# Attention, dense layer and expert layer on one Trainium2 core: one copy of the rows, activations split from products, a fourth output tile, an earlier list stage, another start-up

## The chip, the cores and the metric

The kernel runs on one core of one Trainium2 (trn2) chip. The metric is the device time of one execution in microseconds (us); the median of the runs counts. Engines are named as in the profile: PE is TensorE (matmuls; PEld its weight loads), DVE is VectorE, ACT is ScalarE, POOL is GpSimd, SP is SyncE, which issues nearly all transfers.

## The reference

8 batches of 8 heads, 576 tokens, head size 64; then 4608 tokens of width 512.

```
k_p, v_p = k, v averaged over groups of 8 tokens            # 72 keys a head
attn = softmax(q @ k_p.T / 8) @ v_p                         # 4608 x 512 after joining heads
h = attn @ w_in;  g = where(h > 0, h, exp(min(h, 0)) - 1)   # 512 -> 2048
x = g @ w_out                                               # 2048 -> 512
e = argmax(x @ w_gate);  p = softmax(x @ w_gate)[e]         # 8 experts
out = p * (relu(x @ w1[e]) @ w2[e])                         # 512 -> 1024 -> 512, only expert e of each token
```

## The kernel before, in words

**Products in three terms.** Nearly every float32 factor is cut into a high part (a cast to fp32r) and a low part (the rest), and a product is three matmuls: high by high, low by high, high by low. The cuts are work for ACT (the cast) and DVE or POOL (the subtraction): `w_hi`, `w_lo` for the dense weights, `split` in `m_split` for the experts' weights, `hh`/`hl` for the experts' activations, `zh`/`zl` for gathered rows.

**Attention and dense layer** (about 0 to 1017 us). 12 blocks of 384 tokens go through 16 steps each; a step is 12 matmuls of 128x384 into `h` (`g1_mm`, line 442), the activation over ACT and DVE (`elu_a`, `elu_b`, `elu_c`; lines 452 to 467) and 9 matmuls of 128x512 into `y` (line 484). The attention of later tiles is placed between these by a table of slots: `at(n, slot, fn)` puts a call into step n at a named slot of `step`, and every engine follows the written order. At the start two blocks run interleaved while weights are loaded, decoded (`w_bits`, `w_lo`) and keys and values of the first batches are averaged (`prep_k`, `pool_sum`, `k_scale`; `prep_v2_pool` on POOL). When a block is done, its rows `yr` (512 values and a gate weight) are ready, its 24 gate products are spread over the following steps (`route_at`: a list of how many `r_logit` a step, with `r_gate_load` of the next row of the gate matrix on SP), then `r_top`, `r_weight` (softmax, and the rows are written to DRAM by SP), `r_place` (places in the experts' lists). For blocks 0 to 9 the rows are written twice, to `ybuf` and to `yfirst`; the first five expert units gather from `yfirst`, the later ones from `ybuf`.

**Expert stage** (about 1017 us to the end). The lists of tokens by expert are cut into units: D of 512 tokens (4 tiles of 128), S of 256, T of 128, U of 32. Main units are D0 to D7, T0, T1, S0, T2, four steps each (i = 0 to 3, a quarter of the hidden width); small U units go beside three of them. `mix(n)` writes one step. For a D unit: `m_g1`, 48 matmuls of 128x256 into two banks `mh` and, in the same function, the activations `hh` (ACT, line 1149) and `hl` (DVE, line 1150); `ahead(n)`, a planner that emits the loads (`m_load`: `w1st`, `w2st`, 512 KB each, on SP) and cuts (`m_split`: two ACT casts of 128x1024, two DVE subtractions) of the weights of coming steps as space comes free; `turn_rows`, transposes `zT` of the gathered rows of the next unit (line 1077) with `zh`/`zl`; `m_g2` of the step before (24 matmuls of 128x512 into four banks `my`, and after its last quarter the outputs `o`, scaled by the gate and scattered); `trans_late`, two more transposes; `ahead(n)` again; then the `chores` of the last block: `logits` (4 of its 24 products a step over six steps), `r_top`, `r_weight` (whose three `ybuf` writes SP issues), `r_count`, `r_put`, `lists_rest`, `lists_part`, and `index` (`m_index`: SP reads a value and issues small loads of row numbers). Output tiles `o` are a ring of 3 (line 1176 and after), and each is held until its scatter to `out` has landed.

Of the kernel before, what the change touches and what calls it, by code (L numbers as in the profile page):

```python
# [88 lines left out]
def fused_kernel(ctx: ExitStack, tc: tile.TileContext, q, k, v, w_in, w_out, w_gate, w1, w2, cst, out):  # L89
# [8 lines left out]
    yfirst = dpool.tile([NA, ROW], F32, name="yfirst")  # L98
# [136 lines left out]
    def w_lo(n, c):  # L235
        nc.vector.tensor_sub(w_half(n, c, 1), decs.pop((n, c)).bitcast(F32), w_half(n, c, 0))
        if f"dec{n}_{c}" in slot_w:
            w_free(f"dec{n}_{c}")
# [327 lines left out]
    def r_weight(blk):  # L566
        lg = lgs.pop(blk)
        mx, mb, eq = tops.pop(blk)
        yr = yrows[blk]
        pool = lpool["p"] if blk == NBLK - 1 else mrpool  # L570

        def small_tile(shape, tag, dtype=F32):
            return pool.tile(shape, dtype, tag=tag, name=f"{tag}{blk}")

        se = mrpool.tile([P, TB], F32, tag="rse", name=f"rse{blk}")
        nc.vector.tensor_reduce(se, lg, axis=AX.X, op=ALU.add)
        nc.vector.tensor_scalar_add(se, se, 1e-9)
# [12 lines left out]
        routed[blk] = oh, [small_tile([P, TB, NE], "rpe"), small_tile([P, TB], "rpf"), small_tile([P, TB], "rpi", I32)]  # L590
# [42 lines left out]

    def score_at(t, n, slot="pe_mid"):
# [7 lines left out]
        at(n, "end", s_norm, t)  # L642
# [23 lines left out]
    for b in range(2, B):  # L666
# [6 lines left out]
        for h in range(H):  # L673
            x = n0 - 5 + h if b > 2 else n0 - 4 + min(h, 6)
            at(x - 2, "end", v_load, b, h)
            at(x, "end", prep_v, b, h)

    for n, t in enumerate(range(TB, 2 * TB)):
# [7 lines left out]
        for hh in range(2):  # L686
            at(n + 1, "pe_mid", t_mm, t, hh)
            at(n + 1, "act_hi", t_copy, t, hh, (nc.scalar.copy, nc.vector.tensor_copy)[hh])
# [8 lines left out]
    for n in range(2):  # L697
        w = n + 1
        at(n, "dve_first", w_bits, w, 0)
        at(n, "act_hi", w_hi, w, 0)  # L700
        at(n, "bits", w_bits, w, 1)
        at(n, "bits", w_lo, w, 0)
        at(n, "act_end", w_hi, w, 1)
        at(n, "act_end", w_lo, w, 1)
# [25 lines left out]
    def route_at(blk, n0, per):  # L730
# [3 lines left out]
        for x in range(NE * TB):  # L734
            e, j = divmod(x, TB)
            at(n0 + n, ("dve_mid", "end", "end")[x - sum(per[:n])], r_logit, blk, e, j)
# [20 lines left out]
    def step(n):  # L757
# [6 lines left out]
        elu_a(blk, f)  # L764
        run(n, "act_hi")
# [22 lines left out]
    def first_block():  # L788
# [262 lines left out]
    def m_row(it, u):  # L1051
# [3 lines left out]
        else:  # L1055
# [4 lines left out]
            in_=(yfirst if early_rows(it) else ybuf)[:, :],  # L1060
# [3 lines left out]

    def zf_tag():
        k = turns["zf"] = 1 - turns.get("zf", 0)
        return ("yr", "wgb1")[k]

    def m_trans(it, u):
# [8 lines left out]
        if kind in "TU":  # L1078
            z = mrpool.tile([P, KC, P], F32, tag=zf_tag(), name=f"zf{kind}{s}")
# [50 lines left out]

    def m_g1(it, i):
# [21 lines left out]
    def m_g2(it, i):  # L1153
# [21 lines left out]
        w_free(*(x for x in w_done.pop((it, i)) if x in slot_w))  # L1175
        if i == 3:
            for u in range(nu):
                o = ring(pools[1], [P, DM], F32, "o", 3, f"o{kind}{s}_{u}")
# [36 lines left out]
    def u_trans(it):  # L1215
# [5 lines left out]
        hT = pools[1].tile([P, 2, P], F32, tag="uT", name=f"uTs{s}")  # L1221
# [3 lines left out]
    def u_g2(it):  # L1225
# [15 lines left out]
        o = pools[1].tile([P, P], F32, tag="uo", name=f"uo{s}")  # L1241
# [100 lines left out]
    def logits(n):  # L1342
        for x in range(4 * n, 4 * n + 4):
# [14 lines left out]
    def index(x):  # L1358
        for it in (main[x], side.get(x)):
            if it:  # L1360
                m_index(it)
                m_bound(it)

    def mix(n):
        k, i = seq[n]
        it = main[k]
        if n:
            m_g1(it, i)
            ahead(n)
        for it2, u in trans_at.get(n, ()):  # L1370
            turn_rows(it2, u)
        if n >= 1:
            k0, i0 = seq[n - 1]
            m_g2(main[k0], i0)
# [7 lines left out]
        if n == 14:  # L1382
            for x in range(KD, KD + 3):
                index(x)
            m_gather(side[KD])
        if k >= 4 and i == 1 and k + 4 < len(main):
            index(k + 4)

    ENGINES = {E.PE, E.Activation, E.DVE, E.Pool, E.SP}
    with tc.manual_schedule(engines=ENGINES):  # L1390
        m_g1(main[0], 0)
        for b2, f2 in pend:
            g2(b2, f2)
        y_evac(last)
# [3 lines left out]
    with tc.manual_schedule(engines=ENGINES):  # L1398
# [81 lines left out]
```

## Time and profile before

| | us |
|---|---|
| three runs | 1553.57, 1555.94, 1559.24 (median 1555.94) |
| the profiled execution | 1548.99, span 1547.1 |
| PE busy | 1431.8 (93%), x8834 |
| DVE busy | 969.3 (63%) |
| ACT busy | 739.2 (48%) |
| POOL busy | 127.3 (8%) |
| mean granted TensorE clock | 0.966 |

The span is the time from the first to the last instruction. PE works through its instructions in the written order, so that a wait of one matmul is a hole in the span; the waits of PE with what ended them, and the stretches with a lowered granted clock (1 is 2.4 GHz, 0.5 is 1.2 GHz), are what a change of the order of work can win or lose. A busy share of another engine says little by itself: DVE can be idle on average and late at one place.

### The profile page before, as it was taken

How to read it: one execution, taken by the hardware profiler on the slowest of the kernel's cores; microseconds unless marked ns; L12 is line 12 of the kernel's file. 1: busy time of each engine (PE TensorE's matmuls, PEld its weight loads, DVE VectorE, ACT ScalarE, POOL GpSimd, SP SyncE). 2: the span in 40 equal slices, each digit the busy share in tenths (PEclk: the TensorE clock that was granted, in tenths of full speed). 3: DMA queues.
4: the chain of work that ended last, by engine and by line, in shares of the span. 5: the costliest groups of instructions: out<-in, count | busy, mean ns of one | idle time of the engine just before them, and what ended most of it. 6: DMA issues, size and time to landing. Idle time of an engine off the chain costs nothing. (4 is left out here: it accounts for less than half of the span.)

```text
span 1547.1 us, 24285 instructions
## 1 busy us (share of the span) xinstructions
PE 1431.8 (93%) x8834; PEld 1254.1 (81%) x8834; DVE 969.3 (63%) x2235; ACT 739.2 (48%) x1778; POOL 127.3 (8%) x129
## 2 busy tenths in 40 slices
PE   7899889879999999999999999998888798898988
PEld 4698778768887888887888888897877697877877
DVE  7999777776675777685768576945444533324251
ACT  5677645345655555554656555622223223223241
POOL 1000000000000000000000000202012112112010
PEclk9899999999999999999999999999999899999999
DMA  9245225475545271736281625644464344747460
GB/s 291 73 156 191 87 72 81 95 99 65 77 85 69 81 90 55 79 85 71 72 94 54 75 42 62 179 87 132 128 174 105 101 167 158 247 153 263 158 204 26
DMA packets 108738, 177.27 MB, mean 115 GB/s; under 512 B 15101, under 2 KB 46335, under 8 KB 108608
## 3 DMA queue, kind: packets, MB, share of 16 engines
q1 hardware_dynamic: 101200, 155.65, 44.7%
q0 software_dynamic: 7408, 19.97, 3.9%
q8 instruction: 71, 1.16, 0.4%
q14 instruction: 59, 0.48, 0.2%
HBM read 146.28 MB, written 29.76 MB: 114 GB/s over the span
## 5 line engine op out<-in xcount | busy, mean ns | idle before, releaser
L484 PE MATMUL y<-woh,gh 128*128 128x512 f32 x576 | 235.4, 409 | 2.6 <-ACT yr L500 1.4
L484 PE MATMUL y<-wol,gh 128*128 128x512 f32 x576 | 228.6, 397 | 0.0
L484 PE MATMUL y<-woh,gl 128*128 128x512 f32 x576 | 228.2, 396 | 0.0
L442 PE MATMUL h<-xh,wih 128*128 128x384 f32 x768 | 174.3, 349 | 20.7 <-DVE g L460 19.1
L535 DVE SCALAR_TENSOR_TENSOR junk<-yr,wgb 128x512 bf16<-128x512 f32 x264 | 180.8, 685 | 18.1 <-DMA wgb<-in_moe_w_gate_dram 15.4
L459 DVE SCALAR_TENSOR_TENSOR g<-g,th 128x384 f32<-128x384 f32 x192 | 106.4, 554 | 112.8 <-ACT th L454 111.8
L466 ACT CAST gh<-g 128x384 fp32r<-128x384 f32 x192 | 98.8, 514 | 159.6 <-DVE g L460 141.0
L442 PEld LDWEIGHTS h<-xh,wih 128*128 128x128 f32 x768 | 138.9, 193 | 42.8 <-DVE g L460 21.2
L1149 ACT ACTIVATE hhD<-mhD 128x512 fp32r<-128x512 f32 x64 | 38.3, 598 | 277.9 <-PE myD L1168 269.8
L442 PE MATMUL h<-xl,wih 128*128 128x384 f32 x768 | 169.0, 343 | 0.0
L1150 DVE SCALAR_TENSOR_TENSOR hlD<-mhD,hhD 128x512 fp32r<-128x512 f32 x64 | 44.0, 690 | 198.4 <-ACT hhD L1149 190.9
L442 PE MATMUL h<-xh,wil 128*128 128x384 f32 x768 | 167.7, 341 | 0.0
L452 ACT ACTIVATE th<-h 128x384 f32<-128x384 f32 x192 | 94.3, 491 | 150.6 <-PE h L442 148.7
L442 PEld LDWEIGHTS h<-xl,wih 128*128 128x128 f32 x768 | 139.7, 193 | 0.2
L442 PEld LDWEIGHTS h<-xh,wil 128*128 128x128 f32 x768 | 139.6, 192 | 0.0
L467 DVE TENSOR_TENSOR gl<-g,gh 128x384 fp32r<-128x384 f32 x192 | 107.1, 558 | 42.8 <-ACT gh L466 38.1
L484 PEld LDWEIGHTS y<-woh,gl 128*128 128x128 f32 x576 | 108.8, 189 | 26.0
L484 PEld LDWEIGHTS y<-woh,gh 128*128 128x128 f32 x576 | 109.2, 190 | 24.5 <-DVE yr L502 2.0
L484 PEld LDWEIGHTS y<-wol,gh 128*128 128x128 f32 x576 | 109.1, 189 | 17.5
L611 POOL DMA_INDIRECT tab<-toki,rpi x36 | 37.4, 1039 | 932.8 <-DVE rpi L609 452.4
L1168 PE MATMUL myD<-m2hD,hhD 128*128 128x512 f32 x256 | 103.4, 404 | 7.9 <-DVE gateU L1074 2.9
L460 DVE TENSOR_TENSOR g<-g,h 128x384 f32<-128x384 f32 x192 | 106.3, 554 | 6.6
(272 smaller groups left out, 2483.2 us busy)
## 6 DMA issues: line engine op xcount, KB each, us to landing
wgb<-in_moe_w_gate_dram SPq DMA_DIRECT2D x96, 256.0 KB
w1stD<-in_moe_w_dram SPq DMA_DIRECT2D x32, 512.0 KB
w2stD<-in_moe_w_dram SPq DMA_DIRECT2D x32, 512.0 KB
kst<-in_k_dram SPq DMA_DIRECT2D x32, 288.0 KB
qT<-in_q_dram SPq DMA_DIRECT2D x36, 256.0 KB
ybuf<-yr SPq DMA_DIRECT2D x33, 256.5 KB
raw<-in_moe_w_in_dram SPq DMA_DIRECT2D x16, 512.0 KB
raw<-in_moe_w_out_dram SPq DMA_DIRECT2D x15, 512.0 KB
```

Of the source, the lines that this page charges most:

```text
L442: mark["g1"] = nc.tensor.matmul(ps, wi[i][a][:, c, o:o + P], bb[blk][:, c, :], start=n == 0, stop=n == 3 * KC - 1).ins
L452: nc.scalar.activation(th, hps[blk, f], AF.Relu, scale=-1.0)
L459: nc.vector.scalar_tensor_tensor(g, g, 1.0, th, op0=ALU.add, op1=ALU.mult)
L460: nc.vector.tensor_max(g, g, hps.pop((blk, f)))
L466: nc.scalar.copy(gh, g)
L467: nc.vector.tensor_sub(gl, g, gh)
L484: nc.tensor.matmul(ys[blk][j], a[:, js], wo[i][bb][:, o, :], start=n == 0 and f in FIRST[blk], stop=n == 2 and f in LAST[blk],)
L535: nc.vector.scalar_tensor_tensor(junk, yrows[blk][j][:, :DM], 1.0, pes[blk, e], op0=ALU.mult, op1=ALU.mult, accum_out=lgs[blk][:, j, e:e + 1])
L611: nc.gpsimd.indirect_dma_start(out=tab[:, :], out_offset=bass.IndirectOffsetOnAxis(ap=pi[:, j:j + 1], axis=0), in_=toki[:, TB * blk + j:TB ...
L1149: nc.scalar.activation(hh, ps, AF.Relu)
L1150: nc.vector.scalar_tensor_tensor(hl, ps, 0.0, hh, op0=ALU.max, op1=ALU.subtract)
L1168: nc.tensor.matmul(yps[it][u], a[:, o, us], second[w][:, o], start=i == 0 and o == 0 and n == 0, stop=i == 3 and o == 1 and n == 2,)
```

## The change

- `yfirst` and its writes (27 from `yr`, 3 from `part`) go; the early units gather from the first rows of `ybuf`.
- In the expert stage `m_act` (`hh`, `hl`) is split from `m_g1` and `m_out` (`o`, scatter) from `m_g2`. A step of `mix` is now: `m_g1`, `turn_rows`, `ahead`, `m_g2` of the step before, `m_act`, late transposes, `m_out`. 
- The ring of `o` has 4 tiles; `hT` and `uo` of the U units move to the slots of `yr`, `zf` keeps one slot.
- The chores: 6 logits a step over four steps, `r_top` in step 4, `r_weight` (with the writes) in step 5, `r_place` in 6, `lists_rest` in 8, `lists_part` in 9 to 12; `m_index` of the five units stands at the start of step 13, `m_bound` in 14, the first U gather in 16.
- In the dense part: half of the second batch's key sums and four `w_lo` go to POOL, 10 `warm` matmuls are added in step 1, parts of the weight decoding change places, `s_norm` of tiles 6 and 8 stands earlier in its step, some loads of values come earlier, and `route_at` has other lists, in which most rows of the gate matrix are loaded further ahead of their use.

```diff
-    yfirst = dpool.tile([NA, ROW], F32, name="yfirst")
...
+    def prep_k_pool(b, pr):
+        st = kst.pop((b, pr)).rearrange("p (n j) -> p n j", j=POOLW)
+        t = w_tile([P, SP, POOLW // 2], F32, f"kp{b}_{pr}")
+        nc.gpsimd.tensor_add(t, st[:, :, 0:4], st[:, :, 4:8])
+        nc.gpsimd.tensor_add(t[:, :, 0:2], t[:, :, 0:2], t[:, :, 2:4])
+        nc.gpsimd.tensor_add(kTs[b % 2][:, pr].unsqueeze(2), t[:, :, 0:1], t[:, :, 1:2])
+        w_free(f"kst{b}_{pr}", f"kp{b}_{pr}")
...
-            for dst in (ybuf, yfirst) if blk < NBLK - 2 else (ybuf,):
-                nc.sync.dma_start(dst[r:r + P, :], yr[j])
+            nc.sync.dma_start(ybuf[r:r + P, :], yr[j])
...
-        at(n, "end", s_norm, t)
+        at(n, "dve_mid" if t in SCORE0 else "end", s_norm, t)
...
+        if n == 0:
+            at(1, "pe_mid", warm, 10)
+            at(1, "pe_mid", w_free, "zeros")
...
-    for pr in range(4):
-        at(0, "end", prep_k, 1, pr)
-    at(0, "end", k_scale, 1)
+    for pr in range(2, 4):
+        at(0, "bits", prep_k, 1, pr)
+    at(0, "bits", k_scale, 1)
...
-        at(n, "bits", w_lo, w, 0)
-        at(n, "act_end", w_hi, w, 1)
-        at(n, "act_end", w_lo, w, 1)
+        at(n, "act_end" if n == 0 else "act_mid", w_lo, w, 0, nc.gpsimd)
+        m, slot = (1, "act_first") if n == 0 else (n, "act_end")
+        at(m, slot, w_bits, w, 1)
+        at(m, slot, w_hi, w, 1)
+        at(m, slot, w_lo, w, 1, nc.gpsimd)
...
-    route_at(1, 30, [2, 2] + [3] * 6 + [2])
-    route_at(0, 40, [2, 2] + [3] * 6 + [2])
-    for blk in range(2, last):
+    route_at(1, 30, [1, 2, 2, 2, 2, 3, 3, 3, 3, 3])
+    route_at(0, 41, [2, 2] + [3] * 6 + [2])
+    route_at(2, 3 * NF + LAG + 1, [2, 2, 2, 2, 3, 3, 3, 3, 4])
+    for blk in range(3, last):
         route_at(blk, NF * (blk + 1) + LAG, [3, 2, 3, 2, 3, 2, 3, 2, 2, 2])
...
-            in_=(yfirst if early_rows(it) else ybuf)[:, :],
+            in_=ybuf[:NA if early_rows(it) else NTOK, :],
...
+            mps[it, i, v] = ps
+
+    def m_act(it, i):
+        kind, s = it
+        n = P if kind == "T" else ST
+        for v in range((TILES[kind] + 1) // 2):
+            ps = mps.pop((it, i, v))
             hh = ring(pools[0], [P, 2, n], F32R, "hh", 2, f"hh{kind}{s}_{i}_{v}")
             hl = ring(pools[0], [P, 2, n], F32R, "hl", 2, f"hl{kind}{s}_{i}_{v}")
             nc.scalar.activation(hh, ps, AF.Relu)
...
-                o = ring(pools[1], [P, DM], F32, "o", 3, f"o{kind}{s}_{u}")
+                o = ring(pools[1], [P, DM], F32, "o", 4, f"o{kind}{s}_{u}")
...
-        for x in range(4 * n, 4 * n + 4):
+        for x in range(6 * n, 6 * n + 6):
...
-    chores = {n: [(logits, n)] for n in range(6)}
-    chores[6] = [(r_top, last)]
-    chores[7] = [(r_weight, last)]
-    chores[8] = [(r_count, last)]
-    chores[9] = [(r_put, last)]
-    chores[10] = [(lists_rest,)]
+    chores = {n: [(logits, n)] for n in range(4)}
+    chores[4] = [(r_top, last)]
+    chores[5] = [(r_weight, last)]
+    chores[6] = [(r_place, last)]
+    chores[8] = [(lists_rest,)]
     for j in range(4):
-        chores[11 + j] = [(lists_part, j)]
+        chores[9 + j] = [(lists_part, j)]
...
+        if n == 13:
+            for x in range(KD, KD + 3):
+                index(x, m_index)
         if n:
             m_g1(it, i)
-            ahead(n)
         for it2, u in trans_at.get(n, ()):
             turn_rows(it2, u)
-        if n >= 1:
+        if n:
+            ahead(n)
             k0, i0 = seq[n - 1]
             m_g2(main[k0], i0)
+        if n:
+            m_act(it, i)
+        for it2, u in trans_late.get(n, ()):
+            turn_rows(it2, u)
+        if n:
+            m_out(main[k0], i0)
         if k in side:
             (m_trans_side, u_g1, u_trans, u_g2)[i](side[k])
-        for it2, u in trans_late.get(n, ()):
-            turn_rows(it2, u)
         ahead(n)
```

The order of ACT at the third step of unit D0 (index 2) and its fourth, before. `hhD_2_0` is the activation of step 2 for the first half of the tokens; `m1hD_0` and `m2hD_0` are the weight casts for the next unit's step 0; `zhD` the rows of D1:

```order
L1149 ACTIVATE hhD_2_0_10757<-mhD_2_0_10732 128x512
L1149 ACTIVATE hhD_2_1_10786<-mhD_2_1_10761 128x512
L120 CAST m1hD_0_10803<-w1stD_0_10799 128x1024
L120 CAST m2hD_0_10807<-w2stD_0_10801 128x1024
L1149 ACTIVATE hhD_3_0_10872<-mhD_3_0_10847 128x512
L1149 ACTIVATE hhD_3_1_10901<-mhD_3_1_10876 128x512
L120 CAST m1hD_1_10909<-w1stD_1_10905 128x1024
L120 CAST m2hD_1_10913<-w2stD_1_10907 128x1024
L1088 CAST zhD_0_10924<-zTD_0_10919 128x4x128
L1088 CAST zhD_0_10924<-zTD_1_10931 128x4x128
```

The same place in the change:

```order
L119 CAST m1hD_0_10793<-w1stD_0_10789 128x1024
L119 CAST m2hD_0_10797<-w2stD_0_10791 128x1024
L1171 ACTIVATE hhD_2_0_10825<-mhD_2_0_10730 128x512
L1171 ACTIVATE hhD_2_1_10829<-mhD_2_1_10755 128x512
L1101 CAST zhD_0_10906<-zTD_0_10901 128x4x128
L1101 CAST zhD_0_10906<-zTD_1_10913 128x4x128
L119 CAST m1hD_1_10926<-w1stD_1_10922 128x1024
L119 CAST m2hD_1_10930<-w2stD_1_10924 128x1024
L1171 ACTIVATE hhD_3_0_10958<-mhD_3_0_10849 128x512
L1171 ACTIVATE hhD_3_1_10962<-mhD_3_1_10874 128x512
```

The two weight casts, which wait for their loads, now stand ahead of the activations of the same step instead of behind them, and the first rows' casts `zhD_0` ahead of both; DVE's subtractions follow the same order.

The order of SP at the start of the expert stage, before (`wgb` is a row of the gate matrix for the last block, `w1stD_0`, `w2stD_0` the weights of D1's step 0):

```order
L528 DMA wgb_3_10726<-in_moe_w_gate_dram 128x512
L1095 TENSOR_LOAD l7w
L1095 ISA x2
L1102 ISA
L1102 DMA w1stD_0_10799<-in_moe_w_dram 128x4x256
L1109 ISA
L1109 DMA w2stD_0_10801<-in_moe_w_dram 128x2x512
L528 DMA wgb_4_10837<-in_moe_w_gate_dram 128x512
L528 DMA wgb_5_10845<-in_moe_w_gate_dram 128x512
```

The same place in the change:

```order
L535 DMA wgb_3_10626<-in_moe_w_gate_dram 128x512
L535 DMA wgb_4_10720<-in_moe_w_gate_dram 128x512
L535 DMA wgb_5_10728<-in_moe_w_gate_dram 128x512
L1108 TENSOR_LOAD l7w
L1108 ISA x2
L1115 ISA
L1115 DMA w1stD_0_10789<-in_moe_w_dram 128x4x256
L1122 ISA
L1122 DMA w2stD_0_10791<-in_moe_w_dram 128x2x512
```

Gate rows 4 and 5, each of which is issued when the products with the row two before it are done, stand ahead of D1's first weights now. The three `ybuf` writes of the last block moved in the same way from ahead of D2's third load to ahead of its first, and the small loads of `m_index` from ahead of D4's second load to ahead of D3's fourth.

The order of POOL in the start-up of the change (before it, `tri` and `toki` follow the sums of values directly, and the DMA of the places is next):

```order
L302 TENSOR_TENSOR kT_98<-kp_1_417 128x72
L249 CAST tri<-tri_st 128x128
L251 CAST toki<-small 128x36
L235 TENSOR_TENSOR wil_425<-dec_0_426,wih_424 128x512
L235 TENSOR_TENSOR wil_425<-dec_1_428,wih_424 128x512
L235 TENSOR_TENSOR wol_476<-dec_0_477,woh_475 128x512
L235 TENSOR_TENSOR wol_476<-dec_1_479,woh_475 128x512
```

The four `w_lo` stand behind the copy of `tri`, which waits for a load.

## Rows read from the trace of the kernel before

**Rows 1.** Waits of PE: us in total, times, longest us.

```profile
PE zTD L1077 <- issue: 29.1, 5, 11.0
PE h L442 <- DVE g L460: 19.1, 6, 6.4
...
PE pv L415 <- ACT aT L406: 7.3, 4, 4.4
PE sp L370 <- DVE kT L300: 6.5, 1, 6.5
PE myT L1168 <- DVE hlT L1150: 5.5, 1, 5.5
PE uy L1233 <- issue: 4.5, 1, 4.5
PE myT L1168 <- DVE gateD L1074: 4.2, 1, 4.2
...
PE myD L1168 <- DVE gateU L1074: 2.9, 1, 2.9
PE myD L1168 <- ACT oD L1181: 2.5, 1, 2.5
PE myD L1168 <- DVE oD L1183: 2.5, 2, 2.3
```

**Rows 2.** Waits of DVE, same columns.

```profile
DVE v L283 <- DMA vst<-in_v_dram: 35.5, 5, 9.3
...
DVE oD L1183 <- DMA out_dram<-oD,oidxD: 28.9, 6, 8.0
```

**Rows 3.** The page, costliest group: busy, mean ns | idle before, releaser.

```profile
L535 DVE SCALAR_TENSOR_TENSOR junk<-yr,wgb 128x512 bf16<-128x512 f32 x264 | 180.8, 685 | 18.1 <-DMA wgb<-in_moe_w_gate_dram 15.4
```

**Rows 4.** Windows behind waits: from:to, us; busy; granted clock, DMA share, GB/s.

```profile
228.12:234.00 5.88, 5.88 (x33) 5.31 (x34) 5.16 (x14) 2.21 (x5) 0.00 (x0) 0.71 0.34 69
...
715.13:722.00 6.87, 6.87 (x23) 6.28 (x24) 5.00 (x11) 5.97 (x18) 0.97 (x1) 0.63 0.06 12
...
1058.80:1066.00 7.20, 7.20 (x51) 7.20 (x52) 4.76 (x13) 1.17 (x2) 3.85 (x4) 0.81 0.55 162
...
1343.00:1350.00 7.00, 7.00 (x87) 6.62 (x88) 2.04 (x5) 1.54 (x3) 3.99 (x5) 0.62 0.42 136
...
1373.00:1381.00 8.00, 8.00 (x52) 4.94 (x53) 3.74 (x6) 2.86 (x4) 1.97 (x2) 0.62 0.36 113
...
1495.10:1503.00 7.90, 7.15 (x35) 5.96 (x35) 5.59 (x9) 1.80 (x3) 0.88 (x1) 0.79 0.73 270
```

**Rows 5.** Timeline of POOL and DVE in the start-up: start, us, [idle].

```profile
17.04 1.46 POOL L320 TENSOR_TENSOR vp<-vst 72x512 f32<-72x512 f32 x1
...
17.28 1.25 DVE L392 TENSOR_SCALAR sm<-sm 128x8 f32<-128x8 f32 x1
...
37.77 2.72 DVE L283 TENSOR_REDUCE kT<-kst 128x72 f32<-128x576 f32 x4
```

**Rows 6.** Timeline of SP and ACT, loads of D1: start, us, [idle].

```profile
1034.60 0.39 SPq L1102 DMA_DIRECT2D w1stD<-in_moe_w_dram  x1
...
1042.00 0.60 ACT L1149 ACTIVATE hhD<-mhD 128x512 fp32r<-128x512 f32 x1 [2.20 <-PE myD L1168]
...
1043.80 1.05 ACT L120 CAST m2hD<-w2stD 128x1024 fp32r<-128x1024 f32 x1 [0.26 <-DMA w2stD<-in_moe_w_dram]
```

**Rows 7.** The same, a load behind the last rows' writes.

```profile
1117.03 0.68 SPq L1102 DMA_DIRECT2D w1stD<-in_moe_w_dram  x1
...
1131.48 1.04 ACT L120 CAST m1hD<-w1stD 128x1024 fp32r<-128x1024 f32 x1 [5.01 <-DMA w1stD<-in_moe_w_dram]
```

**Rows 8.** The same, loads behind the row numbers.

```profile
1217.90 1.80 SPq L1031 DMA_DIRECT2D oidxU<-tab  x4
...
1225.44 0.39 SPq L1102 DMA_DIRECT2D w1stD<-in_moe_w_dram  x1
...
1228.91 1.04 ACT L120 CAST m1hD<-w1stD 128x1024 fp32r<-128x1024 f32 x1 [6.03 <-DMA w1stD<-in_moe_w_dram]
```

More of the change, by code (lines that the diff above doesn't have):

```diff
@@ L233, in w_hi, with w_lo @@
         nc.scalar.copy(w_half(n, c, 0), decs[n, c].bitcast(F32))
-    def w_lo(n, c):
-        nc.vector.tensor_sub(w_half(n, c, 1), decs.pop((n, c)).bitcast(F32), w_half(n, c, 0))
+    def w_lo(n, c, eng=None):
+        (eng or nc.vector).tensor_sub(w_half(n, c, 1), decs.pop((n, c)).bitcast(F32), w_half(n, c, 0))
         if f"dec{n}_{c}" in slot_w:
@@ L674, in fused_kernel @@
             x = n0 - 5 + h if b > 2 else n0 - 4 + min(h, 6)
-            at(x - 2, "end", v_load, b, h)
-            at(x, "end", prep_v, b, h)
+            late = b == 3 and h > 3
+            at(n0 - 3 + (h - 3) // 2 if late else x - 2, "end", v_load, b, h)
+            at(n0 - 2 + h // 2 if late and h < 7 else x, "end", prep_v, b, h)
     for n, t in enumerate(range(TB, 2 * TB)):
@@ L687, in fused_kernel @@
             at(n + 1, "pe_mid", t_mm, t, hh)
-            at(n + 1, "act_hi", t_copy, t, hh, (nc.scalar.copy, nc.vector.tensor_copy)[hh])
+        if n == 0:
+            at(1, "pe_mid", warm, 10)
+            at(1, "pe_mid", w_free, "zeros")
+        for hh in range(2):
+            at(n + 1, "act_hi" if n else "act_first", t_copy, t, hh, (nc.scalar.copy, nc.vector.tensor_copy)[hh])
         at(n + 1, "pe_end", pv_mm, t)
         at(n + 1, "copies", pv_copy, t)
-    for pr in range(4):
-        at(0, "end", prep_k, 1, pr)
-    at(0, "end", k_scale, 1)
+    for pr in range(2, 4):
+        at(0, "bits", prep_k, 1, pr)
+    at(0, "bits", k_scale, 1)
     at(1, "end", v_tile, 1)
@@ L735, in route_at @@
             e, j = divmod(x, TB)
-            at(n0 + n, ("dve_mid", "end", "end")[x - sum(per[:n])], r_logit, blk, e, j)
+            at(n0 + n, ("dve_mid", "end", "end", "end")[x - sum(per[:n])], r_logit, blk, e, j)
             if j == TB - 1 and e + 2 < NE:
@@ L764, in step @@
         elu_a(blk, f)
+        run(n, "act_first")
         run(n, "act_hi")
@@ L877, in first_block @@
             w_load(3, c)
+        for pr in range(2):
+            prep_k_pool(1, pr)
         nc.sync.dma_start(small, cst[:, C_W:C_END])
@@ L1078, in m_trans @@
         if kind in "TU":
-            z = mrpool.tile([P, KC, P], F32, tag=zf_tag(), name=f"zf{kind}{s}")
+            z = mrpool.tile([P, KC, P], F32, tag="wgb1", name=f"zf{kind}{s}")
             nc.scalar.copy(z, ps)
@@ L1175, in m_g2, with m_out @@
         w_free(*(x for x in w_done.pop((it, i)) if x in slot_w))
+    def m_out(it, i):
+        kind, s = it
+        nu = TILES[kind]
         if i == 3:
             for u in range(nu):
-                o = ring(pools[1], [P, DM], F32, "o", 3, f"o{kind}{s}_{u}")
+                o = ring(pools[1], [P, DM], F32, "o", 4, f"o{kind}{s}_{u}")
                 gate = gates[it][:, u:u + 1]
@@ L1220, in u_trans @@
             nc.tensor.transpose(ps[:, u], h[:, u * P:(u + 1) * P], ident)
-        hT = pools[1].tile([P, 2, P], F32, tag="uT", name=f"uTs{s}")
+        hT = mrpool.tile([P, 2, P], F32, tag="yr", name=f"uTs{s}")
         nc.vector.tensor_copy(hT, ps)
@@ L1240, in u_g2 @@
         w_free(*(f"t{y}{k}{s}_{i}" for i in range(4) for y, k in (("1", "U"), ("2", ""))))
-        o = pools[1].tile([P, P], F32, tag="uo", name=f"uo{s}")
+        o = mrpool.tile([P, P], F32, tag="yr", name=f"uo{s}")
         nc.scalar.mul(o, ps, gates[it][:, 0:1])
@@ L1347, in logits, with index @@
                 r_gate_load(last, e + 2)
-    chores = {n: [(logits, n)] for n in range(6)}
-    chores[6] = [(r_top, last)]
-    chores[7] = [(r_weight, last)]
-    chores[8] = [(r_count, last)]
-    chores[9] = [(r_put, last)]
-    chores[10] = [(lists_rest,)]
+    chores = {n: [(logits, n)] for n in range(4)}
[3 more added lines that the diff above has]
+    chores[8] = [(lists_rest,)]
     for j in range(4):
-        chores[11 + j] = [(lists_part, j)]
-    def index(x):
+        chores[9 + j] = [(lists_part, j)]
+    def index(x, *fns):
         for it in (main[x], side.get(x)):
-            if it:
-                m_index(it)
-                m_bound(it)
+            for fn in fns:
+                if it:
+                    fn(it)
     def mix(n):
@@ L1383, in mix @@
             for x in range(KD, KD + 3):
-                index(x)
+                index(x, m_bound)
+        if n == 16:
             m_gather(side[KD])
         if k >= 4 and i == 1 and k + 4 < len(main):
-            index(k + 4)
+            index(k + 4, m_index)
+        if k >= 4 and i == 3 and k + 4 < len(main):
+            index(k + 4, m_bound)
     ENGINES = {E.PE, E.Activation, E.DVE, E.Pool, E.SP}
@@ L1393, in fused_kernel @@
             g2(b2, f2)
+        m_act(main[0], 0)
         y_evac(last)
@@ L1406, in fused_kernel @@
         m_g2(main[k0], i0)
+        m_out(main[k0], i0)
     def alone(it):
```

13 lines of the change are left out of this document (6 added, 7 removed).

## The prediction, made before the changed kernel was timed

> **What bounds the kernel now.** I read the page first: PE is busy for 93% of the span (the table above) in the written order of its instructions, and no other engine is near that, so the time is PE's work plus the holes in it. Next come the waits of PE [rows 1]. They fall into four families, each with its own place and cause. (a) `h` of the dense layer waits for DVE's `g`, 19.1 us in six holes, four of which make 18.1 (4.2, 6.4, 3.7 and 3.8, one each behind the end of a block). (b) At the end of the first expert units PE stands before the transposes `zT`, five times and 29.1 us in all: four of 4.5 and one of 11.0; the wait before `uy`, 4.5, is of the same kind. They bear the word "issue" because the profile shows no releaser, but the banks that the transposes write are read by `zh` and `zl`, which on ACT and DVE stood behind the activations and behind the weight cuts of the same step. (c) In the late units `my` waits for DVE's work, 5.5, 4.2 and 2.9. (d) Single ones: `oD` 2.5 and 2.3, `pv` 4.4, `kT` 6.5.
>
> Third come the waits of DVE [rows 2], which tell what (a) and (c) hang on. For (c), `oD` waited 28.9 us for the scatter of an earlier `oD`: the ring of three tiles. For (a), two of the four holes have DVE waiting up to 9.3 us for a load of values, and the other two for a row of the gate matrix [rows 3]: transfers queued behind the six row writes at the end of a block. Last, the windows that begin where PE resumes [rows 4]: PE runs without a hole there, but at a granted clock of 0.61 to 0.81 on average, a mix of the two levels 1.2 and 2.4 GHz. Each hole is paid twice, first as idle time, then as slow matmuls.
>
> **The change, part by part.** I cost a slow stretch as (1 - clock) times the window.
>
> *Dense part.* The 27 second writes of `yr` halve what stands in the queue at each block's end, and the gate rows are asked for earlier. The holes of (a) were smaller than DVE's waits: the longest wait, 9.3, against the longest hole, 6.4, leaves 2.9 that other work covered. A load behind three such writes took 14.5 us elsewhere (below); with three of six gone I take some 7 off the wait, and what remains, 2.3, is covered. The 18.1 us go, and with them `pv`'s 4.4, where DVE stood before a gate row too. The five slow stretches behind them cost from 1.7 (0.29 x 5.88, the first) to 2.5 (0.37 x 6.87, the last), 12.1 together [rows 4]. Dense gain: 18.1 + 4.4 + 12.1 = 34.6.
>
> *Start-up.* Two of the four key sums, 0.68 each (2.72 for four) [rows 5], leave DVE, and four `w_lo`, 128x512 subtractions that I price like the 128x512 of line 535 at 0.69 [rows 3]: 4.1 us less on DVE, whose work has no hole where `kT`'s 6.5 arises. Against it: ten POOL operations run beside DVE, and the first `w_lo` stands behind the copy of `tri` on POOL, which waits for a load. The nearest row for that is a DVE operation of 128x8 elements that began at 17.28 and took 1.25 us, ending at 18.53, while POOL's 128-wide sum ran from 17.04 to 18.50 [rows 5]; a small operation of that sort cannot need a microsecond, so it stood until POOL was through. If each of ten POOL operations held DVE up for half of some 1.2 us, 6 us were lost; if none did, 4.1 are won, and `kT`'s hole bounds the gain at 6.5. I take +2 and keep -2 and +6 for the range. The Trainium skill, SBUF — State Buffer (section SBUF: two separate sides), speaks against this move: VectorE and GpSimd share one port pair, which is locked for a whole instruction, and the other engine blocks. By that rule the start-up would end at -2 and the forecast 4 us later; the row of 1.25 agrees with it, though it shows one case and not how often operations meet.
>
> *Ends of the expert units.* `zh`, `zl` of the first two tiles now stand ahead of everything else of the step, those of the last two behind the activations but ahead of `oD`. The four holes of 4.5 (29.1 - 11.0 = 18.1) and `uy`'s 4.5 should go, 22.6 us, and five slow stretches, from 1.4 (0.19 x 7.20) to 2.7 (0.38 x 7.00), 9.3 together [rows 4]. In exchange two transposes stand ahead of `uy` in one step: about one cast and subtraction, 1.5. Gain 30.4. The hole of 11.0 is treated below.
>
> *Ring of four.* (c) goes: 5.5 + 4.2 + 2.9 = 12.6, and three slow stretches, 3.0 (0.38 x 8.00) to 1.7 (0.21 x 7.90), 6.4 together. DVE's waits of up to 8.0 for a scatter shrink by the time between two uses of one more tile. Gain 19.0.
>
> *Earlier row writes.* (d)'s two waits for `oD`, 2.5 + 2.3, arose when ACT stood 5.0 us for a weight load that was issued at 1117.03, behind the last block's writes, and used at 1131.48 [rows 7]. There it goes: 4.8.
>
> *What is late next.* The weight cuts now stand ahead of the activations on ACT and DVE, and a cut waits for its load. So every load that is late now stops PE, where before it had a step's slack. Three loads become late.
> - D1's first. Before, SP issued it at 1034.60, behind gate row 3, whose turn comes after the second product of step 1. Now it stands behind gate row 5, after the sixth: four products of 0.69 and the reading of their sums later, about 3.1 us. Its second half was used at 1043.80 after a wait, so it lands at 1046.9 now; one cast (1.05), the activation (0.60) and the subtraction behind it (as long again) end at about 1049.1, and PE needs the bank at about 1042.0, where the activation ended the step before [rows 6]. New hole: 7.1, with a slow stretch of 2.4 (the mean of the five dense ones). D1's next load stands behind gate rows 6 and 7, two products: 1.5 more.
> - D2's first, behind the three row writes that now come two steps earlier. From issue to use such a load took 14.5 us, 5.0 of it as a wait of ACT [rows 7]; now a cast (1.0) and this wait come ahead of the activations: 6.0 and 2.4.
> - D3's fourth, behind the row numbers. SP was held from 1217.90 to 1225.44 by these, and the cut then waited till 1228.91 [rows 8]; PE's 11.0 came from that. The same chain now stands one load earlier, with the cut ahead of the activations: I take the same 11.0 and the same stretch, so that the old hole is neither won nor lost.
>
> Together 9.5 + 1.5 + 8.4 = 19.4. Every price here is a load's time from issue to use, and the rows have 3.5 [rows 8], 8.6 [rows 6] and 14.5 us [rows 7]: between these ends I took for each place the row of that place. The Trainium skill, DMA: Bandwidth & Descriptors (Anatomy of one DMA), gives about 2 us and the bytes at 436 GB/s, an estimate of 3.2 us for 512 KB; by it D1's hole would shrink to some 3 us and the forecast would be about 7 us earlier. The 3.5 agrees, the other two rows do not, and those are at the places concerned.
>
> The writes saved, the moved value loads and `s_norm` of two tiles I cost at nothing beyond this: they are covered by PE's work.
>
> **Sum.** 34.6 + 2 + 30.4 + 19.0 + 4.8 - 19.4 = 71.4. The profiled execution took 1548.99, so 1477.6 for such an execution. The median of the runs lies 7.0 us above it; the forecast for the median is 1484.6, rounded 1484.
>
> **Rivals.**
> - *The loads come in time.* Loads of the quiet kind (3.5 us), and fewer writes in the queue: the 19.4 do not arise, and the index hole goes with 11.0 and 2.8. 1484 - 33 = 1451. For it: the row of 3.5, and the saved writes. Against it: SP's order, which puts these loads later than before.
> - *Late loads are worse.* D1's load takes 14.5 instead of 8.6 (+5.9), D2's stays as far behind the writes and waits its full time (+5), and two of the four dense holes stay, since the gate rows alone keep the queue full (+14): 1509. For it: ACT's and DVE's waits at each place where writes and loads meet.
> - *Slower: the cuts ahead of the activations stop every step.* The place is ACT's queue in each of the 48 main steps; the price is what a load misses its turn by. If it is ACT's 5.0 [rows 7], half of it reaching PE (2.5, as in the wait for `oD`), then 48 x 2.5 = 120: 1604. It decides from 29 such steps (71.4 / 2.5). Against it: ACT still waited 2.2 us for PE ahead of the activation at 1042.00 [rows 6], about what two casts take, and most loads are issued a step or more ahead.
> - *The change does not do what it says.* The dense holes hang on the loads themselves and not on the writes, and the late transposes still wait for their banks, because the cuts follow them on DVE: 34.6 and half of 30.4 are lost, 1534. For it: "issue" names no releaser.
>
> **How the numbers follow.** Forecast 0.54, loads in time 0.17, worse loads 0.15, change not doing what it says 0.05, slower 0.09 (of which 0.02 lie near no change). The range holds the forecast with its unknown start-up (4 us either way) and both neighbours: from 1451 less 4 to 1509 plus 4 and one more late load of D1's size (7), 1447 to 1520; what is left out is the slower case and the one at 1534. Faster by over 0.3% (about 5 us, what the runs of this kernel can tell from no change): 0.91; within it 0.02; slower 0.07.
>
> **What would show it.** In the profile after: no wait of `h` for `g` over 2 us, `zT` "issue" gone from the list of PE's waits, `oD` no longer waiting for a scatter; granted clock of the span up from 0.966 to about 0.98. New: PE waits for DVE's `hl` or `mh` in D0's and D1's steps, with ACT waiting for `w1st` or `w2st` just before. If ACT shows these waits in most steps, the slower case holds; if it shows none, the faster one. The forecast is wrong in its main term if the dense holes are still there without the second writes.

## The result, and the profile after

The changed kernel takes 1484.57 us (median of four runs, 1482.19 to 1485.89) against 1557.59 for the kernel before in the same series: a ratio of 0.9532, 95% interval 0.9506 to 0.9558. The forecast was 1484, with a range of 1447 to 1520. The profiled execution took 1484.07 us, its span 1482.3.

To see where the time went I cut the span at two rows of DVE that both kernels have 192 of, the first operation of `elu_b` (`g` from `g` and `th`; line 459 before, 466 after). The third ends the start-up, the last the dense part. Before they begin at 57.7 and 1010.0, after at 63.6 and 986.6 (the rows of these operations, with shortest, median and longest in ns and the start of the first and the last, and the third of them; before, then after):

```profile
L459 DVE SCALAR_TENSOR_TENSOR g<-g,th x192: 544/556/595, 33.2 to 1010.0; 128x384 f32<-128x384 f32 x192
57.71 0.55 DVE L459 SCALAR_TENSOR_TENSOR g<-g,th 128x384 f32<-128x384 f32 x1
```

```profile
L466 DVE SCALAR_TENSOR_TENSOR g<-g,th x192: 543/556/597, 37.5 to 986.6; 128x384 f32<-128x384 f32 x192
63.63 0.55 DVE L466 SCALAR_TENSOR_TENSOR g<-g,th 128x384 f32<-128x384 f32 x1
```


| profiled execution | start-up | dense part | expert stage |
|---|---|---|---|
| before | 57.7 | 952.3 | 537.1 |
| after | 63.6 | 923.0 | 495.7 |
| difference | +5.9 | -29.3 | -41.4 |
| predicted | -2 | -34.6 | -34.8 |

So the sum is near, while the parts are not all so: the start-up went the wrong way. The busy times from the page and the waits of PE after (us in total, times, longest), with which [rows 1] compare:

```profile
PE 1414.8 (95%) x8842; PEld 1243.7 (84%) x8844; DVE 967.1 (65%) x2229; ACT 740.9 (50%) x1778; POOL 146.0 (10%) x139
```

```profile
PE mhD L1159 <- DVE hlD L1172: 24.2, 4, 10.8
PE pv L422 <- ACT aT L413: 10.6, 8, 3.1
PE aTp L407 <- DVE s L401: 6.8, 5, 2.0
PE h L449 <- DVE g L467: 3.8, 3, 2.7
PE sp L377 <- DVE xl L436: 3.0, 1, 3.0
...
PE uy L1259 <- DVE gateD L1087: 1.0, 1, 1.0
```

The waits of `zT` (29.1 before), of `my` for DVE (12.6) and for `oD` (5.0) are not in the list at all; `h` for `g` fell from 19.1 to 3.8, of which 2.7 are one hole in the start-up. One new row carries nearly what is left: `mh` waits 24.2 us for `hl`, in four holes. These are the three late loads and the follower that the prediction named. Their chain, from the timelines of SP, ACT and PE (start, us, idle before and releaser), for D1's first weights, D2's first and D3's fourth:

```profile
1014.30 0.40 SPq L1115 DMA_DIRECT2D w1stD<-in_moe_w_dram  x1
...
1020.71 1.04 ACT L119 CAST m1hD<-w1stD 128x1024 fp32r<-128x1024 f32 x1 [12.60 <-DMA w1stD<-in_moe_w_dram]
...
1024.97 1.23 PE L1159 MATMUL mhD<-zhD,m1hD 128*128 128x256 f32 x4 [6.02 <-DVE hlD L1172]
```

```profile
1065.44 1.32 SPq L589 DMA_DIRECT2D ybuf<-yr  x3
1067.96 0.39 SPq L1115 DMA_DIRECT2D w1stD<-in_moe_w_dram  x1
...
1077.33 1.04 ACT L119 CAST m1hD<-w1stD 128x1024 fp32r<-128x1024 f32 x1 [13.12 <-DMA w1stD<-in_moe_w_dram]
...
1081.58 1.22 PE L1159 MATMUL mhD<-zhD,m1hD 128*128 128x256 f32 x4 [6.54 <-DVE hlD L1172]
```

```profile
1168.90 0.36 SPq L1050 DMA_DIRECT2D oidxT<-tab  x1
1169.51 0.39 SPq L1115 DMA_DIRECT2D w1stD<-in_moe_w_dram  x1
...
1173.02 1.04 ACT L119 CAST m1hD<-w1stD 128x1024 fp32r<-128x1024 f32 x1 [15.69 <-DMA w1stD<-in_moe_w_dram]
...
1177.79 1.22 PE L1159 MATMUL mhD<-zhD,m1hD 128*128 128x256 f32 x4 [10.77 <-DVE hlD L1172]
```

In each, SP issues the load behind the transfers named in the prediction (gate rows, row writes, row numbers), ACT waits 13 to 16 us for it before the cast, and PE resumes 4 to 5 us after the cast begins, when the second cast and the activations are through. From issue to use the three loads took 6.4, 9.4 and 3.5 us.

### The profile page after: what moved, and what is told of

It is laid out like the page before. It is cut to its first block, busy times and chain, and to the rows that moved or that the text cites. A ratio compares the mean times of both kernels' runs of the same rounds, so it can differ in the third digit from the quotient of the medians.

```text
span 1482.3 us, 24237 instructions
## 1 busy us (share of the span) xinstructions
PE 1414.8 (95%) x8842; PEld 1243.7 (84%) x8844; DVE 967.1 (65%) x2229; ACT 740.9 (50%) x1778; POOL 146.0 (10%) x139
## 5 line engine op out<-in xcount | busy, mean ns | idle before, releaser
L449 PE MATMUL h<-xh,wih 128*128 128x384 f32 x768 | 171.2, 345 | 5.4 <-DVE g L467 3.8
L491 PEld LDWEIGHTS y<-woh,gl 128*128 128x128 f32 x576 | 108.7, 189 | 26.1
L1159 PE MATMUL mhD<-zhD,m1hD 128*128 128x256 f32 x512 | 85.9, 291 | 24.3 <-DVE hlD L1172 24.2
```

Source lines behind the costliest of these rows:

```text
L449: mark["g1"] = nc.tensor.matmul(ps, wi[i][a][:, c, o:o + P], bb[blk][:, c, :], start=n == 0, stop=n == 3 * KC - 1).ins
L491: nc.tensor.matmul(ys[blk][j], a[:, js], wo[i][bb][:, o, :], start=n == 0 and f in FIRST[blk], stop=n == 2 and f in LAST[blk],)
L1159: mark["g1"] = nc.tensor.matmul(ps[:, o], a[:, c, o * P:(o + 1) * P], x[:, c], start=k == 0, stop=k == len(terms) - 1).ins
```

## Experiments

The series have their own runs of the kernel before (medians 1553.8 to 1558.3), so I compare ratios; the parts of the profiled span, cut as above, tell the place. What an untouched part differs by between kernels is a measure of chance: the expert stage is 495.6 to 496.2 in four kernels that have it as in the changed kernel (but 537.1 and 542.2 in before and e2, which also have nearly the same one), the dense part 916.6 to 923.9 in the eleven with one set of writes and the new lists, the start-up less steady (below).

| kernel | median | ratio to before | start-up | dense | expert |
|---|---|---|---|---|---|
| changed | 1484.57 | 0.9532 (0.9506 to 0.9558) | 63.6 | 923.0 | 495.7 |
| e1 two writes | 1518.55 | 0.9760 (0.9715 to 0.9805) | 63.2 | 960.0 | 496.2 |
| e2 before, one write | 1527.43 | 0.9811 (0.9770 to 0.9852) | 58.1 | 927.0 | 542.2 |
| e3 old start-up | 1474.73 | 0.9492 (0.9433 to 0.9550) | 57.6 | 920.4 | 496.1 |
| e4 cuts behind | 1468.12 | 0.9444 (0.9409 to 0.9478) | 60.5 | 921.7 | 478.3 |
| e5 ring of three | 1488.09 | 0.9577 (0.9536 to 0.9619) | 60.5 | 919.3 | 505.1 |
| e6 row numbers behind | 1467.59 | 0.9446 (0.9405 to 0.9487) | 60.2 | 922.1 | 483.3 |
| e7 e3 and e4 | 1457.78 | 0.9396 (0.9349 to 0.9443) | 57.5 | 919.8 | 474.4 |
| e8 start-up on DVE | 1480.16 | 0.9526 (0.9486 to 0.9566) | 60.5 | 922.1 | 495.6 |
| e9 e7, planner from T0 on | 1458.03 | 0.9381 (0.9339 to 0.9423) | 57.6 | 916.6 | 479.2 |
| e10 e7, warm matmuls | 1457.92 | 0.9365 (0.9322 to 0.9409) | 58.1 | 923.9 | 474.7 |
| e11 gate rows behind | 1477.72 | 0.9498 (0.9435 to 0.9561) | 63.1 | 922.8 | 490.7 |
| e12 rows' casts behind | 1496.93 | 0.9613 (0.9561 to 0.9664) | 60.8 | 922.1 | 511.6 |

**The second writes** (e1 puts them back into the changed kernel, e2 takes them out of the one before).

```diff
-            nc.sync.dma_start(ybuf[r:r + P, :], yr[j])
+            for dst in (ybuf, yfirst) if blk < NBLK - 2 else (ybuf,):
+                nc.sync.dma_start(dst[r:r + P, :], yr[j])
```

> The changed kernel with the second copy of the rows written again (and gathered from by the first five units). Theory: the dense holes hang on the writes, so PE waits again for g behind the ends of blocks, four holes of about 4 us with slow stretches of 2.5: about 28 us more, 1512. Rival: the earlier gate rows and moved loads closed them, and the writes do not matter: at most 5 us more, 1490.

> The kernel before, with the second copy of the rows left out and nothing else changed. Theory of the writes: the four dense holes and their slow stretches go, 28 us less, about 1529. Rival, that the loads themselves come too late: at most 5 us less, above 1550.

e1's dense part is 37.0 us longer than the changed kernel's, e2's 25.3 shorter than before's: the writes it is, on either side. In e1 the holes are back, and one is larger than any before: PE waited 11.7 us for `aT`, since DVE stood 8.3 us before a load of keys and 3.9 before a gate row. PE's waits of e1, then those of e2 of the same line:

```profile
PE pv L423 <- ACT aT L414: 23.1, 9, 11.7
PE h L450 <- DVE g L468: 14.4, 5, 4.1
```

```profile
PE h L441 <- DVE g L459: 0.9, 1, 0.9
```

e2 has the old lists of gate products and old value loads, and its dense part is 927.0 against 923.0. So the rest of what the change does to the dense part is worth some 4 us, less than equal parts differ by (7.3, from 916.6 to 923.9).

**The start-up** (e3 undoes all of it; e8 keeps its order and the warm matmuls, but has the sums and low parts on DVE). A part of e3's edit, then e8's:

```diff
-    for pr in range(2, 4):
-        at(0, "bits", prep_k, 1, pr)
-    at(0, "bits", k_scale, 1)
+    for pr in range(4):
+        at(0, "end", prep_k, 1, pr)
+    at(0, "end", k_scale, 1)
...
-        at(n, "act_end" if n == 0 else "act_mid", w_lo, w, 0, nc.gpsimd)
+        at(n, "bits", w_lo, w, 0)
```

```diff
-        at(n, "act_end" if n == 0 else "act_mid", w_lo, w, 0, nc.gpsimd)
+        at(n, "act_end" if n == 0 else "act_mid", w_lo, w, 0)
...
-        for pr in range(2):
-            prep_k_pool(1, pr)
```

> The changed kernel with the start-up of the kernel before (all key sums and low parts on DVE, no added warm matmuls, the old places of the weight decoding). The prediction held the new start-up to be 2 us better; then this one takes 2 us more, 1486. Rival, by the profile after, in which the second step of the second block comes 5.9 us later than before: POOL's operations hold DVE up and the low parts come late, so undoing it wins 6 us, 1478. Second rival: only the granted clock fell by chance in that profile (4.3 of the 5.9 us arise before any changed instruction of PE); then undoing wins about 1.6 us, 1483.

> The changed kernel with its own order of the start-up and its added warm matmuls, but the key sums and low parts that it gave to POOL on DVE. Theory: POOL holds DVE up (four DVE operations in the profile after took 2.8 us more than their kind, each ending with POOL's) and delivers the low parts late; without POOL the second step of the second block comes at about 59 us instead of 63.6, and the time is some 4 us less, 1480. Rival: the order and the clock are at fault, not POOL: that step at 63 us or later, and no gain, since DVE has 4.1 us more to do.

With the old order the start-up takes 57.5 to 58.1 us in all six kernels that have it (before, e2, e3, e7, e9, e10), with the new order 60.2 to 63.6 in all eight, e8 among them with 60.5. e3's is 6.0 us shorter than the changed kernel's, the first rival's size. But e8's 60.5 lies between the two numbers expected of it, and four kernels with POOL's part lie there too (e4, e5, e6 and e12, 60.2 to 60.8): so it is the order that costs, and not that POOL does the work. By ratio neither e3 nor e8 is apart from the changed kernel (the intervals overlap); the start-up times carry this reading. What the order does is seen in PE's rows of e8 (start, us, idle): the matmuls for the keys no longer wait 6.5 us but 0.4, and behind them opens a hole of 4.3 and one of 3.1, for `g` and for `xl`:

```profile
37.42 0.72 PE L377 MATMUL sp<-kT,qT 64*64 64x72 f32 x28 [0.40 <-DVE kT L307]
...
44.03 1.65 PE L449 MATMUL h<-xh,wih 128*128 128x384 f32 x4 [4.29 <-DVE g L467]
...
53.04 0.70 PE L377 MATMUL sp<-kT,qT 64*128 64x72 f32 x2 [3.07 <-DVE xl L436]
```

DVE's rows show why. In the kernel before it has no hole from the first operation `g`, at 33.2, to the third, 24.5 us later. In e8 the first is at 33.2 too, but the third comes 27.3 us later, and 2.4 of the 2.8 us more are four waits of DVE for ACT. Three are for casts of weights: each low part now stands directly behind the decoding of its own half, and ACT's cast of that half has to come between. The fourth is for `xh` (DVE of e8):

```profile
41.50 0.69 DVE L235 TENSOR_TENSOR wil<-dec,wih 128x512 fp32r<-128x512 f32 x1 [0.68 <-ACT wih L232]
...
46.51 0.69 DVE L235 TENSOR_TENSOR wol<-dec,woh 128x512 fp32r<-128x512 f32 x1 [0.74 <-ACT woh L232]
...
51.25 0.69 DVE L235 TENSOR_TENSOR wol<-dec,woh 128x512 fp32r<-128x512 f32 x1 [0.68 <-ACT woh L232]
52.29 0.69 DVE L436 TENSOR_TENSOR xl<-pv,xh 128x512 fp32r<-128x512 f32 x1 [0.34 <-ACT xh L435]
```

In the changed kernel the same stretch takes 26.1 us: DVE waits 1.1 for `gh` and 1.7 for `xh`, which on ACT stand behind such a cast, and POOL's part gives back 1.1 of e8's 2.8 (the seven kernels with it take 25.1 to 26.2). The other 4.3 of its 5.9 us arise ahead of the first `g`, which begins at 37.5. The added warm matmuls are not the cause in e8: behind them PE still waits 0.4 us for the keys.

A second part is the granted clock. In the changed kernel it is down to 0.57 on average from 20 to 36 us, in e8 and e3 it is 1.00 there (windows, columns as in [rows 4]: the changed kernel, then e8):

```profile
20.00:36.00 16.00, 14.57 (x94) 12.32 (x95) 12.20 (x22) 7.73 (x26) 5.34 (x7) 0.57 0.95 296
```

```profile
20.00:36.00 16.00, 13.45 (x120) 10.72 (x121) 14.79 (x27) 11.01 (x33) 0.05 (x1) 1.00 0.97 287
```

The clock sorts the start-ups too: in the three kernels of 63.1 to 63.6 (changed, e1, e11) it is 0.57 to 0.68 in this window, in the four others with sums on POOL, of 60.2 to 60.8, it is 0.89. All seven profiles with sums on POOL have a fall of the clock before 31 us, one of the other seven (e10) has one. Why is open: in the changed kernel it begins at 22.2, before POOL's first sum at 23.7, PE's holes in the 14 us ahead of it are of 1.2 us at most, as in e3, and e8, which has no sums on POOL, is one profile.

**The cuts and the loads** (e4 moves the planner behind the activations; e6 and e11 leave it ahead and reorder SP's queue alone).

The edits of e4, e6 and e11 (of the last two only the new places):

```diff
         if n:
-            ahead(n)
             k0, i0 = seq[n - 1]
             m_g2(main[k0], i0)
```

```diff
             ahead(n)
+            if n == 13:
+                for x in range(KD, KD + 3):
+                    index(x, m_index)
```

```diff
             ahead(n)
+            while held:
+                r_gate_load(last, held.pop(0))
```

> The changed kernel with the planner's call (loads and cuts of weights) moved from ahead of the activations of a step to behind them, everything else as changed. Theory: the three new holes (6.0, 6.5, 10.8) arise because a cut that waits for its load stands ahead of the activations; they go with their slow stretches (3, 3, 6): 33 us less, about 1451. Rival: the loads are too late for their own use too, and the holes only move by a step: at most 10 us less, above 1474.

> The changed kernel with the row numbers of five units issued behind the loads of step 13 instead of ahead of them; nothing else is moved. Theory: the hole of 10.8 us (and its slow stretch, some 2.5 of matmuls) is D3's fourth weight load behind these small loads on SP: 13 us less, about 1472. Rival: that load is late for want of space or of DMA time, or the row numbers are now late for the first gathers: at most 5 us less, above 1479.

> The changed kernel with gate rows 4 and 5 of the last block issued behind D1's first weights instead of ahead of them; nothing else is moved. Theory, by the prediction's term for D1: the hole of 6.0 us (and 0.9 a step later) goes with its slow stretch: 8 us less, about 1477. Rival: the weights' own transfer is what takes long, so the hole stays above 4 us and the time within 3 us of the changed kernel.

e4 is 0.0088 of before lower than the changed kernel, 13.7 us, its expert stage 17.4 shorter. The mechanism holds: of the holes of 6.0, 6.5 and 10.8 only 1.5 of the last is left, and 1.3 of D1's follower. The size was wrong: I had put their slow stretches at 12, while the clock of the windows behind them (0.70, 0.62, 0.70) makes some 7, and two holes came in their place, 2.8 (a transpose behind `r_place`) and 3.8 (in D7, where ACT waited 7.5 for a load). PE's waits of e4:

```profile
PE mhD L1159 <- DVE hlD L1172: 6.5, 3, 3.8
...
PE zTD L1090 <- DVE rpe L611: 2.8, 1, 2.8
```

e6 moves only the small loads of the row numbers: the hole of 10.8 goes, and 12.4 us of the expert stage with it, as expected (13). The other two stay, 7.4 and 6.6 (PE's waits of e6):

```profile
PE mhD L1159 <- DVE hlD L1172: 14.7, 3, 7.4
```

e11 moves only gate rows 4 and 5: D1's first load is issued at 1001.3 instead of 1014.3, and the hole of 6.0 is gone; but the next load now stands behind four gate rows, and its hole grows from 0.9 to 3.5. Of the expected 8 us the expert stage shows 5.0; by ratio the run is not apart from the changed kernel. So both halves of the theory are needed for a hole: SP's order makes the load late, and the cut's place ahead of the activations hands that on to PE. For D2's hole, behind the row writes, only the second half is tested (e4).

**The ends of the units** (e12).

```diff
             m_act(it, i)
+            z_copies()
```

`z_copies` writes the casts and subtractions of the first two row tiles, whose transposes stay where they are.

> The changed kernel with the casts and subtractions of the first two gathered row tiles put back behind the activations of the step (the transposes stay at their place on PE, and the weight cuts stay ahead). Theory, by the prediction's term for the ends of the units: the late transposes wait for these banks again, five or six holes of about 2.4 us (4.5 less the two casts, which are not behind the activations here): 12 us more plus slow stretches, 1497 to 1502, with zT <- issue or a row copy in PE's waits. Rival: the split of activations and outputs from the products closed those holes, not the place of the rows: at most 4 us more, 1488.

```profile
PE mhD L1170 <- DVE hlD L1183: 24.1, 3, 10.4
PE zTD L1090 <- issue: 11.0, 6, 1.9
```

PE's waits show the old row again, six holes of 1.8, and the expert stage is 15.9 us longer: 11.0 of holes and the slow stretches. "issue" is a bank that waits for its reader. The holes of the kernel before were 2.7 us longer; the two weight casts that stood ahead of the row casts there (1.05 each) fit that, but no run puts them back.

**The ring of output tiles** (e5).

```diff
-                o = ring(pools[1], [P, DM], F32, "o", 4, f"o{kind}{s}_{u}")
+                o = ring(pools[1], [P, DM], F32, "o", 3, f"o{kind}{s}_{u}")
```

> The changed kernel with three output tiles again. Theory: DVE waits for the scatter of an earlier tile in the last units, PE behind it 2.9, 4.2 and 5.5 us with slow stretches of 6.4: 19 us more, 1504. Rival: the outputs stand behind the activations now, so the scatter has more time and a ring of three does as well: at most 5 us more, 1490.

The rival is near: the median's 3.5 us (0.0045 by ratio) are not apart from none. DVE waits for the scatter nearly as before [rows 2], and it no longer reaches PE, which waits 1.4 and 1.2 where it waited 12.6 [rows 1] (waits of DVE, then of PE, of e5):

```profile
DVE oD L1209 <- DMA out_dram<-oD,oidxD: 23.2, 5, 6.8
```

```profile
PE myT L1190 <- DVE gateS L1087: 1.4, 1, 1.4
PE myT L1190 <- DVE gateD L1087: 1.2, 1, 1.2
```

In the kernel before, `oD` belonged to `m_g2` and stood ahead of the activation's `hl` on DVE, so that a late scatter held up the next products; `m_out` stands behind it now. That explanation is read from the order, no run undoes it alone. The expert stage of e5 is 9.4 longer; those two are 2.6 of it, and 6.2 lie in the holes of the late loads (30.4 in that row against 24.2), where no reason from the ring is seen.

**Toward a better kernel** (e7 joins e3 and e4 and puts `r_place` ahead of the planner; e9 and e10 go on from it). e7's further edit, then those of e9 and e10:

```diff
+        if n == 6:
+            r_place(last)
         ahead(n)
```

```diff
         if n:
+            if n >= 28:
+                ahead(n)
```

```diff
+            at(1, "pe_mid", warm, 20)
```

> The changed kernel with the start-up of the kernel before and the planner's call behind the activations together, and the places of the last block (r_place) ahead of the planner in step 6. Theory: the two gains, 9.8 and 16.5 by their own runs, are in different parts and add up, with 2.8 more for the transposes that waited behind r_place: about 1456. Rival: part of them is chance of the granted clock, and they do not add up: above 1464.

> The kernel e7_both with the planner ahead of the activations again from unit T0 on, where steps are short and the weights of four units are loaded at once. Theory: its hole of 3.7 us in D7 (ACT waited 7.5 for a load issued late) goes with a slow stretch of 1.7: 5 us less than e7_both, about 1453. Rival: DMA is the limit there, the load is as late: within 2 us of e7_both.

> The kernel e7_both with 20 warm matmuls (0.23 us each) in the hole of 6.5 us in which PE waits for the second batch's keys, and the old start-up otherwise. Theory: the hole stays as long as DVE's sums, but the slow stretch of 10.2 us behind it (3.4 lost) goes: 3 us less, about 1455. Rival: DVE sets the pace of the start-up and the slow matmuls there are hidden: no change, 1458, and the second step of the second block at 57.5 us as before.

The gains add up: by ratio e3 gains 0.0040 on the changed kernel, e4 0.0088 and e7 0.0136, and the transposes no longer wait behind `r_place`. e7 is faster than the kernel before and the changed one, 0.9396 of before (0.9349 to 0.9443), its interval wholly below the changed kernel's. e9 and e10 are the same as e7 within their intervals, and both rivals hold. In e9 the hole of 3.7 in D7 became one of 7.4. The profile names the row numbers of T2 (`gidxT`) as its end, an operation of 0.14 us on DVE; DVE had stood behind a cast of ACT that waited 7.0 us for its load, issued at 1328.7 and used at 1341.1 (1332.8 and 1343.0 in e7). The DMA engines were busy for nine tenths of that time or more, and with the cut ahead of the activations the wait reaches PE. In e10, with the hole of 6.5 filled but for 2.5, the start-up is 58.1 against 57.5, at DVE's pace. ACT's row of e9:

```profile
1341.14 1.04 ACT L119 CAST m1hD<-w1stD 128x1024 fp32r<-128x1024 f32 x1 [7.02 <-DMA w1stD<-in_moe_w_dram]
```

## Why the prediction was right, and where it was not

- **Where PE stands.** Right: the four families of holes went, but for `pv`, and the three new ones came where and how the text said, with 7.1, 6.0 and 11.0 forecast and 6.0, 6.5 and 10.8 found, and the follower with 0.9 for 1.5. e4, e6 and e11 show the two conditions. In the first, 7.1 rests on a misread row: the activation at 1042.00 [rows 6] begins there and ends at 1042.60, which would have made 6.5.
- **Dense part.** The cause is shown by e1 and e2. Of 34.6 us 29.3 came: the slow stretches of the block ends went, but `pv` did not lose its waits for `aT`; its row went from 7.3 to 10.6 instead of down by 4.4. The hole of 4.4 itself is 4.6 in e2, so it did not hang on the second writes; in the changed kernel there are eight shorter ones, up to 3.1.
- **Start-up.** This step failed. "I take +2" became -5.9. What was counted, work taken off DVE (4.1 us) against what POOL holds up, came near: four DVE operations beside POOL's took 2.8 us more than their kind, and POOL's part left DVE's stretch 1.1 shorter than in e8. What the sum left out was larger. The new order costs 2.8 (e8), since DVE, which had no hole, now waits for ACT's casts: I had not asked what stands next once the hole for the keys is closed. And 4.3 arose ahead of the first `g`, while the granted clock was 0.57, which the start-up's term left out. The Trainium skill, SBUF — State Buffer (section SBUF: two separate sides), has the engines block each other for whole instructions, and the rows agree again (a subtraction of 128x384, 0.57 on average, took 1.63 beside POOL's 1.36), but that price is not what decided: with POOL's part taken away (e8) the start-up stays within the spread of the others. The two rows, of DVE and POOL:

```profile
40.30 1.63 DVE L474 TENSOR_TENSOR gl<-g,gh 128x384 fp32r<-128x384 f32 x1
```

```profile
40.15 1.36 POOL L235 TENSOR_TENSOR wil<-dec,wih 128x512 fp32r<-128x512 f32 x1
```

- **Ends of the units.** Right in cause (e12) and size: holes of 22.6 forecast, all of `zT` gone and 1.6 left at `uy`, for the 1.5 set aside.
- **Ring of four.** PE's 12.6 us went, yet mostly for another reason than the prediction gave: with three tiles only 2.6 of them return. The same change has another cure for this wait by its order (`m_out` behind the activations), and I had credited the ring; that the order did it is not shown.
- **Earlier row writes.** The two waits for `oD`, 2.5 and 2.3, are gone, but here too the split of the outputs from `m_g2` is a rival, and no run takes the two apart.
- **Late loads.** 19.4 forecast, and the price from the row of the place was good to about a microsecond a hole, though the first two loads were quicker from issue to use than the rows that priced them: 7.1 for 8.6 (both for the second load of the pair, which in before was issued at 1035.24) and 9.4 for 14.5. The Trainium skill, DMA: Bandwidth & Descriptors (Anatomy of one DMA), gives the fit, from which the estimate was 3.2 us, for transfers that GpSimd issues, while SP issues these; of the three loads only the third (3.5) is near it.
- **The sum.** 71.4 forecast, 64.9 found between the two profiled executions: the start-up was 8 worse, the dense part 5 worse, the expert stage 6.6 better. That the median hit 1484 is part chance: I added the 7 us by which before's runs lie above its profiled one, and those after lie 0.5 above theirs. By the medians of the series, 1557.59 and 1484.57, the change is worth 73.0.

## What to carry to other kernels

When a change moves work that waits for a transfer ahead of work that waits for nothing, write down every transfer that is queued ahead of it: each late one can become a hole of the bound engine, even if it had a step's slack before, and either side (the queue's order or the place of the waiting instruction) can cure it. Cut the span at rows that both kernels have in equal number before believing that a sum is right, since errors of opposite sign hide in it. Where PE waits for an engine that works without a hole, closing one wait of PE only shows the next, and a new order can give that engine waits of its own (here DVE for ACT's casts): look for both before crediting a gain.

## What was not expected

A hole of PE costs more than its length, and for long ones less than I took in e4 (3, 3 and 6): behind holes of 6.0, 6.5 and 10.8 us the windows in which PE ran again lost 2.1 (0.30 x 7.03), 2.8 (0.38 x 7.42) and 2.5 us (0.30 x 8.21), hardly more than the 1.4 to 2.7 behind holes of 4.5 [rows 4]. The windows of the changed kernel:

```profile
1024.97:1032.00 7.03, 7.03 (x44) 7.03 (x45) 4.72 (x14) 0.00 (x0) 0.00 (x0) 0.70 0.21 61
1081.58:1089.00 7.42, 7.42 (x41) 7.42 (x42) 1.25 (x7) 0.00 (x0) 0.97 (x1) 0.62 0.39 134
1177.79:1186.00 8.21, 8.21 (x49) 8.18 (x50) 2.81 (x3) 1.01 (x2) 0.00 (x0) 0.70 0.77 266
```

And the clock of the start-up differed between kernels whose instructions were alike up to there, by 3 us of time: with sums on POOL ahead it fell early in seven of seven profiles. That is a coincidence to look into, not a cause shown.
